# Attention, feed-forward and routed experts in one kernel: where the first block's weights and keys are made ready

## The chip, the cores and the metric

The kernel runs on one core of a Trainium2 chip. The metric is the device time of one execution in microseconds, the median of three runs. A core has five engines that run side by side, each through its own list of instructions in order: TensorE (PE; matmuls, with weight loads as an own row, PEld), VectorE (DVE), ScalarE (ACT), GpSimd (POOL) and SyncE (SP), which here only issues transfers. Results of matmuls land in PSUM, eight banks of 128 partitions by 512 words; everything else lives in SBUF.

## The reference, cut to what matters

```python
# q, k, v: 8 batches x 8 heads x 576 positions x 64
k_p = k.reshape(B, H, 72, 8, D).mean(axis=3)      # keys and values pooled by 8
v_p = v.reshape(B, H, 72, 8, D).mean(axis=3)
attn = softmax(q @ k_p.T / 8)                     # 576 x 72 for each batch and head
x = heads_joined(attn @ v_p)                      # 4608 tokens x 512
h = x @ w_in                                      # w_in: 512 x 2048
g = where(h >= 1, h, where(h <= -1, 0, (h + 1) ** 2 / 4))
y = g @ w_out                                     # w_out: 2048 x 512
# then each token goes to one of 8 experts (512 -> 1024 -> 512), chosen by y @ w_gate
```

`w_in` and `w_out` arrive as 64-bit floats, so that the kernel makes 32-bit words of them itself.

## The kernel before, in words

The 4608 tokens are 36 tiles of 128. They go through the feed-forward in ten blocks of 3, 4 (seven times), 3 and 2 tiles (`BLK`, L57). While one block is in its products, the attention of the next block's tiles is worked in between, unit by unit, from a list written out by hand (`weave`, L371; `slot`, L1032); the first block's three tiles go through attention ahead of everything (L982 to L1022, the head).

A product that has to be exact is made of three fast ones: each operand is split into a high part in the type `fp32r` and a low part, and high x high, high x low and low x high are added in PSUM. `f1` (L477) makes step m's first product: 12 matmuls into `ps0` or `ps1` (L483 to L485). Then VectorE clips (L490), ScalarE squares (L491), VectorE takes the larger (L495, `larger`), ScalarE copies the high part into `FG` (L496), and VectorE subtracts for the low part (L502, `lower`). `f2` (L505) makes the second product of step m for each tile: three matmuls (L511 to L513) with `FG` against `WO`, added over the 16 steps in banks `ps2` and following. `f1` runs two steps ahead of `f2` (`AHEAD`).

The weights are made ready during the head and the first block. `load_raw` (L403) fetches a slice of 64-bit words (512 KB) into one of six buffers `RB`; in all there are 16 slices of `w_in` and 16 of `w_out` (`order`, L446). A `tick` (L462) moves this on by one slice at each of its three stages. `convert_a` (L421) lets ScalarE scale the upper words into `WOF` or `DFI`. `convert_b` queues three steps for VectorE (`pend`, worked off by `mix`): shift left (L427), put in the lower word's upper bits (L428), put in the sign (L431), all three in SBUF. `convert_c` (L435) lets ScalarE copy the high part (L439) and GpSimd or VectorE subtract for the low part (L227, a helper's line); for `w_out` both parts are also stored to `wo_d` in memory (L442), 512 KB a slice. From the second block on `load_out` (L473) fetches them again for every step.

Keys and values: a batch has 8 slices each of 72 x 512 (144 KB), pooled by `pool_kv` into 72 x 64: one reduction on VectorE (L213) or three additions on GpSimd (L216 to L218). `u_kt` (L241) then turns the pooled keys with TensorE into `KBD`. Batch 0 is pooled in the head; batches from 1 on by `kv_step`, one slice at a time, through three buffers `RAW` that are refilled as they come free.

All transfers except those of `wo_d` into `WO` go through SP's queue in the order of the program; SP stands still at the first whose buffer isn't free.

Of the kernel before, what the change touches and what calls it, by code (L numbers as in the profile page):

```python
# [23 lines left out]
def attention_ffn_routed_experts_kernel(  # L24
# [44 lines left out]

    wo_d = dram.tile([KF, 128, 2, DM], F32R, name="wo_d")  # L70
# [36 lines left out]
    KP = at(4800, 512, SP_)  # L107
    YF = Y.rearrange("p t d -> p (t d)")
# [4 lines left out]
    NRB = len(RB)  # L113
    FR = fx(0, 512)
# [105 lines left out]
    banks = deque(ps[2:8])  # L220
# [16 lines left out]
    def flush():  # L237
        for _ in range(len(later)):
            later.popleft()()

# [116 lines left out]
    def kv_step(b, i):  # L357
        def f():
            n = (b - 1) * 2 * H + i
            pool_kv(b, i, RAW[n % 3], nc.vector)  # L360
            if n + 3 < (B - 1) * 2 * H:
                load_kv(1 + (n + 3) // (2 * H), (n + 3) % (2 * H), RAW[n % 3])
        return f
# [24 lines left out]
    I0 = 24  # L388
# [9 lines left out]
    units.insert(3, [units[3][0], lambda: u_kt(1)])  # L398
# [25 lines left out]
    def convert_b(i):  # L424
        dst, rb = cvt_dst(i)
        di = dst.bitcast(I32).rearrange("p (a x) -> p a x", a=8)
# [21 lines left out]
    n = FIRST  # L448
# [28 lines left out]
    def f1(j, m):  # L477
# [814 lines left out]
```

## Time and profile before

| | before |
|---|---|
| median of 3 runs | 1571.1 us (1569.75 to 1572.26) |
| profiled execution, own time | 1567.33 us |
| its span, first to last instruction | 1565.6 us |
| TensorE busy | 1456.0 us, 93% of the span |
| weight loads busy | 1185.2 us, 76% |
| VectorE busy | 796.5 us, 51% |
| ScalarE busy | 488.0 us, 31% |
| GpSimd busy | 220.2 us, 14% |
| granted TensorE clock, mean | 0.973 |
| transfers | 128 GB/s over the span |

The shares are means over a head, ten blocks of feed-forward (to about 1100 us) and the experts. A busy TensorE need not be one at its peak, as matmuls lie partly beside each other in its records. The granted clock is the share of full speed that the chip gave TensorE; full is 2.4 GHz and the lower level 1.2 GHz. In the rows below an arrow such as `<-DVE FG L502` names what ended an idle stretch.

### The profile page before, as it was taken

Reading aid. Unit: us, or ns where it says so; the run is one execution under the profiler, and the core shown is the slowest. Engines: PE = TensorE matmul, PEld = TensorE weight load, DVE = VectorE, ACT = ScalarE, POOL = GpSimd, SP = SyncE. Lnnn points to the kernel's source line nnn. Section 1 sums busy time; section 2 is a strip of 40 time slices with the busy share of each in tenths; the row PEclk is TensorE's granted clock in tenths of the full one; section 3 lists DMA queues with packets and bytes.
Section 4 is the critical chain, followed back from the end, with each engine's and each line's share of the span. In section 5 each row is a group of like instructions: output and inputs, shape, how many; then the busy total and the mean of one; then the engine's idle time right before and its main releaser. Section 6 shows DMA issues by size and latency. Waiting matters only on the chain.

```text
span 1565.6 us, 19805 instructions
## 1 busy us (share of the span) xinstructions
PE 1456.0 (93%) x7419; PEld 1185.2 (76%) x7419; DVE 796.5 (51%) x1561; ACT 488.0 (31%) x900; POOL 220.2 (14%) x218
## 2 busy tenths in 40 slices
PE   4677799899999999999999999898899999999697
PEld 3566577678778778778778788787788888888585
DVE  6798766545656654664764444434422222212326
ACT  5345332333333333333333333234211111111334
POOL 4222100000101001001000010102222110111112
PEclk9789999999999999999999999999999999999899
DMA  8466336525737637547456265877152110110413
GB/s 227 150 213 206 135 108 123 119 83 128 119 117 120 125 100 101 139 137 91 126 122 99 75 109 106 196 180 137 41 158 72 55 42 26 48 48 28 147 41 142
DMA packets 102631, 177.55 MB, mean 113 GB/s; under 512 B 46610, under 2 KB 54949, under 8 KB 102512
## 3 DMA queue, kind: packets, MB, share of 16 engines
q10 hardware_dynamic: 21552, 75.79, 24.4%
q1 hardware_dynamic: 73392, 79.93, 18.2%
q0 software_dynamic: 7568, 20.33, 4.0%
q8 instruction: 64, 1.05, 0.3%
q14 instruction: 55, 0.45, 0.1%
HBM read 171.32 MB, written 28.29 MB: 128 GB/s over the span
## 4 chain that ended last, share of the span: by engine, by line
PE 77%; DVE 9%; DMA 6%; issue 3%; ACT 2%; POOL 1%; another core or an unknown queue 1%; SPq 0%; ACTq 0%; DVEq 0%; POOLq 0%
PE ps L483 8%; PE ps L511 7%; PE ps L485 7%; PE ps L484 7%; PE ps L513 7%; PE ps L512 7%; PE ps L853 4%; PE ps L854 4%; PE ps L855 4%; PE ps L868 4%; PE ps L869 4%; PE ps L870 4%; PE ps L339 2%; PE ps L284 2%; DVE FX L428 2%
## 5 line engine op out<-in xcount | busy, mean ns | idle before, releaser
L511 PE MATMUL ps<-WO,FG 128*128 128x512 f32 x576 | 242.4, 421 | 23.5 <-ACT WO L439 11.2
L483 PE MATMUL ps<-XT,W 128*128 128x512 f32 (+2 forms) x640 | 252.2, 394 | 12.6 <-DVE FG L502 12.0
L484 PE MATMUL ps<-XT,W 128*128 128x512 f32 (+2 forms) x640 | 240.1, 375 | 3.0 <-DVE XT L345 3.0
L485 PE MATMUL ps<-XT,W 128*128 128x512 f32 (+2 forms) x640 | 240.2, 375 | 0.7 <-POOL W L227 0.7
L491 ACT ACTIVATE FX<-FX,half 128x512 f32<-128x512 f32 (+2 forms) x152 | 104.0, 684 | 418.5 <-DVE FX L490 407.4
L512 PE MATMUL ps<-WO,FG 128*128 128x512 f32 x576 | 230.5, 400 | 3.7 <-POOL WO L227 2.8
L513 PE MATMUL ps<-WO,FG 128*128 128x512 f32 x576 | 229.6, 399 | 0.0
L490 DVE TENSOR_SCALAR FX<-ps 128x512 f32<-128x512 f32 (+2 forms) x152 | 96.5, 635 | 183.0 <-PE ps L485 183.0
L859 DVE SCALAR_TENSOR_TENSOR FG<-ps,FG 128x512 fp32r<-128x512 f32 (+1 forms) x64 | 43.2, 675 | 220.1 <-ACT FG L858 220.1
L511 PEld LDWEIGHTS ps<-WO,FG 128*128 128x128 f32 x576 | 111.0, 193 | 55.0 <-issue 13.7
L483 PEld LDWEIGHTS ps<-XT,W 128*128 128x128 f32 x640 | 123.2, 193 | 36.1 <-DVE FG L502 13.9
L485 PEld LDWEIGHTS ps<-XT,W 128*128 128x128 f32 x640 | 123.1, 192 | 20.7 <-POOL W L227 1.4
L484 PEld LDWEIGHTS ps<-XT,W 128*128 128x128 f32 x640 | 123.6, 193 | 19.9 <-DVE XT L345 3.9
L496 ACT ACTIVATE FG<-ps 128x512 fp32r<-128x512 f32 (+2 forms) x160 | 88.7, 554 | 148.1 <-DVE ps L495 136.8
L512 PEld LDWEIGHTS ps<-WO,FG 128*128 128x128 f32 x576 | 111.2, 193 | 26.0 <-POOL WO L227 4.2
L513 PEld LDWEIGHTS ps<-WO,FG 128*128 128x128 f32 x576 | 110.6, 192 | 25.1
L495 DVE TENSOR_TENSOR ps<-FX,ps 128x512 f32<-128x512 f32 (+2 forms) x152 | 97.4, 641 | 55.6 <-ACT FX L491 54.4
L502 DVE TENSOR_TENSOR FG<-ps,FG 128x512 fp32r<-128x512 f32 (+2 forms) x160 | 100.7, 630 | 39.5 <-ACT FG L496 39.5
L858 ACT ACTIVATE FG<-ps 128x512 fp32r<-128x512 f32 (+1 forms) x64 | 37.4, 584 | 261.8 <-PE ps L855 261.3
L318 POOL TENSOR_TENSOR AT<-AT,ssm 128x576 f32<-128x576 f32 x36 | 42.6, 1186 | 478.9 <-DVE ssm L311 411.1
L853 PE MATMUL ps<-XT,W 128*128 128x512 f32 (+1 forms) x256 | 99.1, 387 | 0.0
L854 PE MATMUL ps<-XT,W 128*128 128x512 f32 (+1 forms) x256 | 98.7, 386 | 0.0
(229 smaller groups left out, 2287.0 us busy)
## 6 DMA issues: line engine op xcount, KB each, us to landing
WO<-wo_d ACTq DMA_DIRECT2D x144, 512.0 KB
AT<-in_moe_w_dram SPq DMA_DIRECT2D x10, 2048.0 KB
AT<-in_moe_w_dram SPq DMA_DIRECT2D x14, 1024.0 KB
AT<-in_v_dram SPq DMA_DIRECT2D x60, 144.0 KB
AT<-in_q_dram SPq DMA_DIRECT2D x32, 256.0 KB
wo_d<-WO SPq DMA_DIRECT2D x16, 512.0 KB
AT<-in_k_dram SPq DMA_DIRECT2D x56, 144.0 KB
yrow_d<-Y SPq DMA_DIRECT2D x7, 1032.0 KB
```

Of the source, the lines that this page charges most:

```text
L483: nc.tensor.matmul(o, wi(m, 0, c), xh, start=(c == 0), stop=False)
L484: nc.tensor.matmul(o, wi(m, 0, c), xl, start=False, stop=False)
L485: nc.tensor.matmul(o, wi(m, 1, c), xh, start=False, stop=(c == KD - 1))
L490: nc.vector.tensor_scalar(r, o, -1.0, 1.0, op0=ALU.max, op1=ALU.min)
L491: nc.scalar.activation(out=r, in_=r, func=ACTF.Square, scale=0.5, bias=half)
L495: nc.vector.tensor_tensor(out=o, in0=r, in1=o, op=ALU.max)
L502: nc.vector.tensor_tensor(out=gl, in0=o, in1=r32(gh), op=ALU.subtract)
L511: nc.tensor.matmul(o, gh, WO[:, g % 4, 0], start=(m == 0), stop=False)
L512: nc.tensor.matmul(o, gh, WO[:, g % 4, 1], start=False, stop=False)
L513: nc.tensor.matmul(o, gl, WO[:, g % 4, 0], start=False, stop=(m == KF - 1))
L853: nc.tensor.matmul(o, e1(0)[:, c, ms], xh, start=(c == 0), stop=False)
L854: nc.tensor.matmul(o, e1(0)[:, c, ms], xl, start=False, stop=False)
```

## The change

In words: keys of batches 0 and 1 are no longer pooled by reductions and then turned; 64 plain fp32 matmuls a batch against the unit matrix (`u_kp`) add and turn them in one, and ScalarE copies the sums into `KBD`. Batch 1's keys come in pairs through two new buffers `PAIR`; its values are pooled on GpSimd. Bank `ps5` becomes `CV`: the word being joined stands there between the three steps of a conversion. For the first block, `larger` writes the activations unsplit (`G32`), the second products are one plain fp32 matmul with the unsplit `WOF`, and `w_out` is neither copied nor split nor stored in two parts: the unsplit 256 KB go to `w32_d`. In the second block each step loads its slice from there, splits it on ScalarE and VectorE, uses it and stores both parts to `wo_d`, from which the third block on reads as before. The head issues its transfers and units in another order, a tick queues VectorE's three steps together with ScalarE's first and finishes a slice two ticks behind instead of three, and batch 2's pooling starts two units later.

```diff
+    w32_d = dram.tile([KF, 128, DM], F32, name="w32_d")
+    PAIR = [at(3264 + 1024 * i, 1024, SP_) for i in range(2)]
+    G32 = [WG.rearrange("p e d -> p (e d)")[:, 3072 + GN * i:3072 + GN * (i + 1)] for i in range(2)]
+    G32.append(at(6336, GN))
-    banks = deque(ps[2:8])
+    CV = ps[5]
+    banks = deque(ps[2:5] + ps[6:8])
+    def u_kp(b, c, raw):
+        pb = bank()
+        raw = raw.rearrange("p (a r d) -> p a r d", a=2, r=8)
+        for r in range(8):
+            for i in range(2):
+                nc.tensor.matmul(pb[64 * i:64 * i + 64, 0:SP_], raw[:, i, r], ident[0:SP_, 0:SP_],
+                                 start=(r == 0), stop=(r == 7))
+        nc.scalar.activation(out=KBD[b][0:64, c, 0:SP_], in_=pb[0:64, 0:SP_], func=ACTF.Copy)
+        nc.scalar.activation(out=KBD[b][64:128, c, SP_:2 * SP_], in_=pb[64:128, 0:SP_],
+                             func=ACTF.Copy)
...
-            pool_kv(b, i, RAW[n % 3], nc.vector)
+            pool_kv(b, i, RAW[n % 3], nc.vector if b > 1 else nc.gpsimd)
+    def load_pair(c):
+        for i in range(2):
+            load_kv(1, 2 * c + i, PAIR[c % 2][:, 512 * i:512 * (i + 1)])
+    def pair_step(c):
+        def f():
+            u_kp(1, c, PAIR[c % 2])
+            if c < 2:
+                load_pair(c + 2)
+            for n in ((9, 10), (8,))[c - 2] if c > 1 else ():
+                load_kv(1, n, RAW[n % 3])
+        return f
-    I0 = 24
+    I0 = 27
-    units.insert(3, [units[3][0], lambda: u_kt(1)])
...
     def convert_b(i):
-        pend.append(lambda: nc.vector.tensor_scalar(di, di, 3, None, op0=ALU.logical_shift_left))
+        di, ci = (x.bitcast(I32).rearrange("p (a x) -> p a x", a=8) for x in (dst, CV))
+        pend.append(lambda: None)
+        pend.append(lambda: nc.vector.tensor_scalar(ci, di, 3, None, op0=ALU.logical_shift_left))
         pend.append(lambda: nc.vector.scalar_tensor_tensor(
-            out=di, in0=rb[:, :, :, 0], scalar=29, in1=di, op0=ALU.logical_shift_right,
+            out=ci, in0=rb[:, :, :, 0], scalar=29, in1=ci, op0=ALU.logical_shift_right,
             op1=ALU.bitwise_or))
         pend.append(lambda: nc.vector.scalar_tensor_tensor(
-            out=di, in0=rb[:, :, :, 1], scalar=-2 ** 31, in1=di, op0=ALU.bitwise_and,
+            out=di, in0=rb[:, :, :, 1], scalar=-2 ** 31, in1=ci, op0=ALU.bitwise_and,
             op1=ALU.bitwise_or))
     def convert_c(i):
-        hi, lo = (WO[:, m % 4, 0], WO[:, m % 4, 1]) if o else (wi4(m, 0), wi4(m, 1))
+        if o:
+            nc.sync.dma_start(out=w32_d[m], in_=dst)
+            return
+        hi, lo = wi4(m, 0), wi4(m, 1)
         nc.scalar.activation(out=hi, in_=dst, func=ACTF.Copy)
-        low_part(lo, dst, hi, nc.vector if o and m % 3 else nc.gpsimd)
-        if o:
-            nc.sync.dma_start(out=r32(wo_d[m]), in_=r32(WO[:, m % 4]))
+        low_part(lo, dst, hi)
     def tick():
-        mix(3)
-        if n > 1:
-            more_raw(n - 2 + NRB)
-        for f, i in ((convert_c, n - 3), (convert_a, n), (convert_b, n - 1)):
+        mix(4)
+        if n > 0:
+            more_raw(n - 1 + NRB)
+        for f, i in ((convert_c, n - 2), (convert_a, n), (convert_b, n)):
+    def load_32(m):
+        nc.scalar.dma_start(out=WOF[m % 4], in_=w32_d[m])
+    def split_out(m):
+        nc.scalar.activation(out=WO[:, m % 4, 0], in_=WOF[m % 4], func=ACTF.Copy)
+    def split_low(m):
+        low_part(WO[:, m % 4, 1], WOF[m % 4], WO[:, m % 4, 0], nc.vector)
+        nc.sync.dma_start(out=r32(wo_d[m]), in_=r32(WO[:, m % 4]))
...
         def larger():
+            if j == 0:
+                nc.vector.tensor_tensor(out=G32[m % 3], in0=r, in1=o, op=ALU.max)
+                if m == KF - 1:
+                    load_32(0)
+                return
             nc.vector.tensor_tensor(out=o, in0=r, in1=o, op=ALU.max)
             nc.scalar.activation(out=gh, in_=o, func=ACTF.Copy)
-            if g + 1 >= KF and g + 1 < len(steps):
+            if j == 1:
+                split_out(m)
+                if m + 1 < KF:
+                    load_32(m + 1)
+            if g + 1 >= 2 * KF and g + 1 < len(steps):
                 load_out(g + 1)
         def lower():
             nc.vector.tensor_tensor(out=gl, in0=o, in1=r32(gh), op=ALU.subtract)
+            if j == 1:
+                split_low(m)
...
     def f2(j, m):
+            if j == 0:
+                nc.tensor.matmul(o, G32[m % 3][:, ts], WOF[m % 4], start=(m == 0), stop=(m == KF - 1))
+                continue
...
-        for i in range(8):
-            head_pool(i, nc.gpsimd if i in (1, 3, 5) else nc.vector)
-        u_kt(0)
+        for c in range(4):
+            u_kp(0, c, wgp[:, 1024 * c:1024 * (c + 1)])
+        load_pair(0)
+        load_pair(1)
-        kv = deque(kv_step(1, i) for i in range(2 * H))
+        kv = deque([pair_step(c) for c in range(4)] + [kv_step(1, i) for i in range(H, 2 * H)])
-        banks.extend(ps[2 + HEAD:8])
+        banks.extend(ps[6:8])
```

## Rows read from the trace of the kernel before

**Rows 1.** Busy time by stretch: us, then each engine, clock, transfers' share, GB/s

```profile
0.00:37.00 37.00, 18.48 (x112) 14.71 (x112) 23.31 (x45) 19.39 (x72) 17.80 (x34) 0.94 0.86 225
37.00:61.00 24.00, 13.55 (x43) 11.83 (x44) 18.23 (x27) 7.30 (x14) 5.51 (x4) 0.57 0.55 164
61.00:190.00 129.00, 99.42 (x508) 79.87 (x507) 111.92 (x193) 56.39 (x108) 32.39 (x30) 0.90 0.57 181
190.00:302.00 112.00, 104.92 (x536) 83.10 (x537) 69.21 (x127) 35.93 (x66) 7.75 (x7) 0.97 0.52 120
256.00:284.00 28.00, 27.38 (x143) 21.60 (x142) 17.81 (x28) 7.71 (x14) 3.11 (x3) 1.00 0.78 86
```

**Rows 2.** The chain of waits, 0 to 330 us, its shares by line

```profile
by line: DVE FX L428 7.7%; DMA AT<-in_v_dram 7.0%; issue 6.3%; DVE AT L213 4.9%; PE ps L483 4.8%; PE ps L485 4.4%; PE ps L484 4.4%; PE ps L511 4.0%; DMA AT<-in_k_dram 3.8%; PE ps L512 3.8%; PE ps L513 3.8%; DVE FX L431 3.7%; DVE FX L427 3.0
```

**Rows 3.** Waits of TensorE, 0 to 345 us: total, times, longest

```profile
PE ps L483 <- DVE FG L502: 12.0, 4, 6.3
PE ps L511 <- ACT WO L439: 11.2, 8, 3.9
```

**Rows 4.** VectorE's groups, 61 to 190 us: busy us, mean ns, idle before

```profile
L427 DVE TENSOR_SCALAR FX<-FX 128x512 int32<-128x512 int32 x25 | 13.0, 521 | 0.0
L428 DVE SCALAR_TENSOR_TENSOR FX<-WG,FX 128x512 int32<-128x512 int32 x12 | 12.4, 1031 | 0.1
...
L213 DVE TENSOR_REDUCE VS<-AT 72x64 f32<-72x512 f32 x8 | 8.4, 1044 | 0.0
L502 DVE TENSOR_TENSOR FG<-ps,FG 128x384 fp32r<-128x384 f32 x15 | 8.2, 546 | 0.0
...
L227 DVE TENSOR_TENSOR WO<-FX,WO 128x512 fp32r<-128x512 f32 x10 | 6.9, 691 | 5.1 <-ACT WO L439 5.1
...
L431 DVE SCALAR_TENSOR_TENSOR FX<-AT,FX 128x512 int32<-128x512 int32 x4 | 2.8, 688 | 0.1
```

**Rows 5.** Single lines of VectorE, 20 to 190 us: ns min/median/max

```profile
L427 DVE TENSOR_SCALAR FX<-FX x32: 405/417/1427, 28.8 to 176.2; 128x512 int32<-128x512 int32 x32
L428 DVE SCALAR_TENSOR_TENSOR FX<-WG,FX x15: 675/692/1741, 43.1 to 167.3; 128x512 int32<-128x512 int32 x15
L345 DVE SCALAR_TENSOR_TENSOR XT<-ps,XT x14: 406/424/425, 28.4 to 177.2; 128x256 fp32r<-128x256 f32 x14
L490 DVE TENSOR_SCALAR FX<-ps x10: 543/548/681, 50.8 to 189.7; 128x384 f32<-128x384 f32 x8, 128x512 f32<-128x512 f32 x2
```

**Rows 6.** Timeline of GpSimd and VectorE near 45 us: start, duration

```profile
45.20 1.71 POOL L227 TENSOR_TENSOR W<-FX,W 128x512 fp32r<-128x512 f32 x1 [3.63 <-ACT W L439]
...
45.81 1.65 DVE L428 SCALAR_TENSOR_TENSOR FX<-WG,FX 128x512 int32<-128x512 int32 x1
```

**Rows 7.** Timeline of TensorE: neighbouring first products, then neighbouring second products

```profile
65.80 0.33 PE L485 MATMUL ps<-XT,W 128*128 128x384 f32 x1
65.97 0.33 PE L483 MATMUL ps<-XT,W 128*128 128x384 f32 x1
...
220.14 0.40 PE L511 MATMUL ps<-WO,FG 128*128 128x512 f32 x1
...
220.38 0.39 PE L512 MATMUL ps<-WO,FG 128*128 128x512 f32 x1
```

**Rows 8.** The gate's line L544, plain fp32, whole span: ns min/median/max

```profile
L544 PE MATMUL ps<-WG,WGT x80: 379/592/597, 218.6 to 1101.0; 128*8 128x512 f32 x56, 128*8 128x384 f32 x16, 128*8 128x256 f32 x8
```

**Rows 9.** Timeline of TensorE, the start of the first block

```profile
37.20 0.69 PE L483 MATMUL ps<-XT,W 128*128 128x384 f32 x1 [0.63 <-ACT XT L344]
...
54.21 0.69 PE L483 MATMUL ps<-XT,W 128*128 128x384 f32 x1 [6.31 <-DVE FG L502]
...
61.16 0.80 PE L511 MATMUL ps<-WO,FG 128*128 128x512 f32 x1
```

**Rows 10.** The chain of waits, 250 to 290 us: start, us, what

```profile
252.59 9.39 DMA AT<-in_k_dram
...
274.90 12.49 DMA AT<-in_v_dram
```

More of the change, by code (lines that the diff above doesn't have):

```diff
@@ L113, in attention_ffn_routed_experts_kernel @@
     NRB = len(RB)
+    GN = blocks[0][1] * 128
+    G32 = [WG.rearrange("p e d -> p (e d)")[:, 3072 + GN * i:3072 + GN * (i + 1)] for i in range(2)]
+    G32.append(at(6336, GN))
     FR = fx(0, 512)
@@ L425, in convert_b @@
         dst, rb = cvt_dst(i)
-        di = dst.bitcast(I32).rearrange("p (a x) -> p a x", a=8)
-        pend.append(lambda: nc.vector.tensor_scalar(di, di, 3, None, op0=ALU.logical_shift_left))
+        di, ci = (x.bitcast(I32).rearrange("p (a x) -> p a x", a=8) for x in (dst, CV))
+        pend.append(lambda: None)
+        pend.append(lambda: nc.vector.tensor_scalar(ci, di, 3, None, op0=ALU.logical_shift_left))
         pend.append(lambda: nc.vector.scalar_tensor_tensor(
-            out=di, in0=rb[:, :, :, 0], scalar=29, in1=di, op0=ALU.logical_shift_right,
+            out=ci, in0=rb[:, :, :, 0], scalar=29, in1=ci, op0=ALU.logical_shift_right,
             op1=ALU.bitwise_or))
         pend.append(lambda: nc.vector.scalar_tensor_tensor(
-            out=di, in0=rb[:, :, :, 1], scalar=-2 ** 31, in1=di, op0=ALU.bitwise_and,
+            out=di, in0=rb[:, :, :, 1], scalar=-2 ** 31, in1=ci, op0=ALU.bitwise_and,
             op1=ALU.bitwise_or))
@@ L968, in attention_ffn_routed_experts_kernel @@
     with tc.manual_schedule():
-        pre = [WG[0:SP_, i] for i in range(8)]
-        raw0 = pre + RAW + [FX[0:SP_, 512 * i:512 * (i + 1)] for i in range(1, 5)] + [JK[0:SP_]]
+        wgp = WG.rearrange("p e d -> p (e d)")[0:SP_]
+        raw0 = [WG[0:SP_, i] for i in range(8)] + RAW + [
+            FX[0:SP_, 512 * i:512 * (i + 1)] for i in range(1, 5)] + [KP]
         nc.scalar.dma_start(out=WGT, in_=w_gate.rearrange("(c p) e -> p c e", p=128))
@@ L984, in attention_ffn_routed_experts_kernel @@
             load_kv(0, i, raw0[i])
+        more_raw(0)
         load_q(1)
-        hu[0][0]()
         for i in range(H, 2 * H):
             load_kv(0, i, raw0[i])
-        for i in range(3):
-            more_raw(i)
-        for i in range(8):
-            head_pool(i, nc.gpsimd if i in (1, 3, 5) else nc.vector)
-        for i in range(8, 13):
-            head_pool(i, nc.gpsimd)
-        for i in range(3):
-            load_kv(1, i, RAW[i])
-        hu[1][0]()
-        u_kt(0)
-        hu[0][1]()
-        hu[0][2]()
-        hu[1][1]()
-        hu[1][2]()
-        for i in range(13, 16):
-            head_pool(i, nc.vector)
-        hu[2][0]()
+        hu[0][0]()
+        more_raw(1)
+        more_raw(2)
+        for c in range(4):
+            u_kp(0, c, wgp[:, 1024 * c:1024 * (c + 1)])
         for i in range(3, NRB):
             more_raw(i)
+        tick()
+        hu[1][0]()
+        for i in (8, 10, 12, 14):
+            head_pool(i, nc.gpsimd)
+        mix(4)
+        head_pool(9, nc.vector)
+        hu[0][1]()
+        head_pool(11, nc.vector)
+        hu[0][2]()
+        head_pool(13, nc.vector)
+        hu[1][1]()
+        head_pool(15, nc.vector)
+        load_pair(0)
+        load_pair(1)
+        hu[1][2]()
+        hu[2][0]()
         flush()
+        tick()
         hu[2][1]()
@@ L1018, in attention_ffn_routed_experts_kernel @@
             flush()
-            if i % 2 == 1 and ticks[0] < CAHEAD + 4:
+            if i % 2 == 1 and ticks[0] < CAHEAD + 3:
                 tick()
-            if i > 3 and kv:
-                kv.popleft()()
-        while ticks[0] < CAHEAD + 4:
+        while ticks[0] < CAHEAD + 3:
             tick()
         banks.clear()
-        banks.extend(ps[2 + HEAD:8])
+        banks.extend(ps[6:8])
         steps = [(j, m) for j in range(NB) for m in range(KF)]
```

## The prediction, made before the changed kernel was run

> **What bounds the kernel now.** I read the engine shares first, then busy time by stretch, then one engine's lines inside the stretch that looked wrong, then who waits for whom there. TensorE is busy 93% of the whole span, but that is an average over unlike stages. By stretch [rows 1] the second block (190 to 302 us) holds TensorE at 104.9 of 112 us, and there only fewer or faster matmuls could help. The first block (61 to 190 us) takes 129 us for three tiles, against 112 us for four, and has TensorE at 99.4, VectorE at 111.9 of 129 and a granted clock of 0.90; the 24 us before it have VectorE at 18.2 and a clock of 0.57. The reader is to see that in these 153 us VectorE is the fuller engine. The chain of waits agrees [rows 2]: over the first 330 us its largest single item is VectorE's L428, with L213, L431 and L427 of the same engine behind it. TensorE's own waits [rows 3] name it again: 12.0 us for FG from L502 and 11.2 us for WO from L439, which itself stands behind VectorE's conversion. So what counts is what the change takes off VectorE before 190 us, and what it adds to TensorE there and to the transfers of the second block.
>
> Times are made against the profiled execution, 1567.33 us with a span of 1565.6; the three runs have a median of 1571.1, which is 3.8 more, and I move the answer by the same difference.
>
> **The change part by part, first block (61 to 190 us).** VectorE [rows 4] (the 27 rows of this view add up to 124 us where the stretch has 111.9 busy, so some 0.07 of each instruction lies beside the next, and I take that off):
> - Values of batch 1 pooled on GpSimd instead: 8 of L213 at 1.044 go, 8 x 0.97 = 7.8 us. Keys of batch 2 start two units later and the inserted key unit is gone; counting the list of units, 5 instead of 8 of them fall into this block: 3 x 0.97 = 2.9 us move to the second block, where VectorE is at 69 of 112.
> - Low halves of the first block's activations (L502) go: 15 x 0.47 = 7.0 us.
> - Low halves of w_out on VectorE (L227) go: 10 x 0.61 = 6.1 us, and the 5.1 us that VectorE stood idle in front of them waiting for ScalarE's copy.
> - Conversions stay, 25 in this stretch (L427, L428 and L431, seven rows by source buffer of which three are shown; busy 13.0 + 12.4 + 7.8 + 2.7 + 9.0 + 8.2 + 2.8 = 55.9 us). What is new is that a PSUM bank holds the word between the three steps. Undisturbed, an L428 takes 0.68 to 0.69, disturbed up to 1.74 [rows 5]. At 45.81 one took 1.65 while GpSimd's L227 ran from 45.20 [rows 6]. L345, the same instruction with one input in PSUM, stayed within 0.406 to 0.425 in all its 14 runs [rows 5]. So steps two and three should stay at their undisturbed 0.68 and 0.69. Step one now writes PSUM. No row shows that; it lies between the 0.417 median of today's form (L427's mean is 0.521 with its disturbed ones) and L490's 0.681 with 512 elements read from PSUM [rows 4, 5]. I take 0.68, the one nearest in kind. That makes 25 x (0.68 + 0.68 + 0.69) = 51.3, a gain of 4.6 us; with the low end for step one it is 11.2, and if PSUM shields nothing and step one still grows, 25 x (0.68 - 0.52) = 4 us are lost.
>
> The sum for VectorE is 7.8 + 2.9 + 7.0 + 6.1 + 5.1 + 4.6 = 33.5, so a stage bound by VectorE as now would last 129 - 33.5 = 95.5 us.
>
> The Trainium skill speaks against this part in "VectorE: DVE Perf Modes", under why PSUM operands drop a tier: one-source fp32 work runs at double rate only from SBUF to SBUF. By that rule step one costs the 0.68 that the row of L490 gave; without it the sum would be 6.6 us better. Its page "SBUF — State Buffer", under who interferes with whom, has a VectorE instruction with one SBUF input and at single rate never wait for GpSimd: by that the 4 us of loss can't come, L345's 14 runs agree, and no row shows an integer step with a word in PSUM.
>
> TensorE in the same stage. Matmuls of 384 columns start 0.17 us apart and of 512 columns 0.23 us apart [rows 7], while a record of the latter lasts 0.40; a record therefore ends some 0.165 us later than its column stream. L544, plain fp32 with 512 columns, has records of 0.592, so a stream of 0.427, and 80 records for 40 products: two each [rows 8]. A second product in plain fp32 should then cost 2 x 0.427 = 0.854 plus the 0.018 per record that the 0.231 spacing has over its own stream, 0.89 us. The three that it replaces take 3 x 0.231 = 0.69. For 16 x 3 products TensorE goes from 33.3 to 42.7 us: it gains work. First products: 16 x 12 x 0.172 = 33.0. Attention: the second block has 104.9 us busy and 16 x 24 x 0.231 = 88.7 in its products, so 16.2 at most for four tiles with the routing. Together 92 us. VectorE's 95.5 and TensorE's 92 now almost meet, and two engines that feed each other do not both run full: between 0 (VectorE's 95.5 already holds its 12 us of idle time) and 16 us (the 17 us that VectorE is idle today, once more) I put 8 on top. The stage then lasts some 103 us: **26 us less**, between 18 and 34.
>
> ScalarE (56.4 of 129 us) loses the copies of WO and FG, and GpSimd (32.4 of 129) takes 8 poolings, each surely under the 1.71 of a full 128x512 [rows 6]; both cost nothing as long as a pooling that waits for its values doesn't keep L227 behind it from the first products. Storing 256 KB instead of 512 KB per step takes 4.2 MB off a queue that moved 181 GB/s here.
>
> **Before the first block (0 to 61 us).** VectorE loses 8 poolings of batch 1's keys (8 x 0.97 = 7.8 us), which stood between the conversions from 29 to 45 us. TensorE gets 64 plain products per batch in their place. What ends last today [rows 9]: first products from 37.2, a hole of 6.31 us until 54.21 waiting for FG from L502, the first second product at 61.16. That hole goes, since a VectorE with less in its queue frees the bank sooner. Late next are batch 1's keys: TensorE now stands at u_kp until each pair has landed, with the value products and the first products of the block queued behind it. Counting on SP's queue up to the last pair: 4 of q (1.05 MB), 16 of batch 0 (2.36), 9 raw blocks (4.7), 8 keys (1.2), together 9.3 MB at the 225 GB/s of the first stretch, 41 us and 2 to 3 for the start: 44 us. Then the rest of the values and three first products at the slow clock, some 9 to 13 us: the first second product at 53 to 57. If only two pairs hold it up it is 49. I take 53: **8 us less**, between 4 and 12. In front of that u_kp(0) waits for keys that land one by one, where pooling on two engines kept pace; I count that inside these bounds, as the softmax of the first tiles still follows the same transfers.
>
> **Second block (190 to 302 us).** Added per step: a load of 256 KB on ScalarE's queue, a copy (0.62), a subtraction on VectorE (0.69) and a store of 512 KB on SP's queue; gone is the 512 KB load. Engines have room: VectorE 69 + 16 x 0.69 + 2.9 = 83 of 112, ScalarE 36 + 10. The transfers are the question. The load is issued one step (7.0 us) before ScalarE's copy waits for it, with the activations of the next step queued behind; before, it had three steps. And SP's stores stand ahead of the keys and values that VectorE pools. In 256 to 284 us the queues moved only 86 GB/s at a busy share of 0.78 [rows 1], 144 KB of keys or values took 9.4 to 12.5 us to land [rows 10], and the wait of TensorE for FG that this block has comes right behind. Per step the demand rises from about 0.9 to 1.15 MB. At 86 GB/s these 28 us carry 2.4 MB, 2.1 steps instead of 4: 13 us lost if nothing is buffered, and some 5 us of slack in the two steps between first and second product. So between -4 (the present hole goes) and +13; I take **4 us more**.
>
> Sum: -26 - 8 + 4 = -30; 1567.3 becomes 1537, and the median of runs 1571.1 - 30 = 1541. Everything after 302 us is the same work.
>
> **Rivals.**
> - TensorE becomes the bound: 92 us of work at the 0.90 clock of today's stage make 102, with the same 8 of friction 110 instead of 103, and the late keys leave 4 instead of 8 of the front: -19 - 4 + 4 = -19, 1552. For it: the plain products. Against it: a fuller engine has held a clock of 0.97 to 1.00 [rows 1].
> - Both engines overlap as well as in the second block and its transfers are hidden: 95.5 in the stage, 49 for the front, nothing lost later: -33.5 - 12 + 2 = -43.5, 1528. For it: two steps of slack between a first product and its use.
> - PSUM shields nothing, so the change doesn't do what it says to the conversions: 8.6 us worse than my sum, 1550. Against it: L345 [rows 5].
> - Slower than before: the second block is paced by its transfers. Place: ScalarE's wait for the unsplit weights, and SP's stores ahead of keys and values. It cancels 34 us of gain when 16 steps take 2.1 us more each, 9.1 instead of 7.0, which is when the queues move less than 1.15 MB / 9.1 us = 126 GB/s. With 86 GB/s over half the block, 8 steps of 13.4 instead of 7.0 lose 51 us: 1571 - 34 + 51 = 1588. For it: the 28 us above. Against it: 181 GB/s and 225 GB/s elsewhere, and 120 GB/s in this block is what it asked for, with a busy share of 0.52.
>
> **How the numbers follow.** Forecast 0.46 (1541, its own range 1531 to 1551); TensorE bound 0.18 (1552); everything overlaps 0.17 (1528); PSUM shields nothing 0.07 (1550); transfers of the second block 0.09, slower; 0.03 for a gain that is eaten just about whole. Faster by over 0.2% (some 3 us, which is what this kernel's runs can tell) 0.88, within it 0.03, slower 0.09. The range from 1522 to 1562 leaves out the slow case and the ends of the others.
>
> **What would show it.** Right: L428's and L431's longest runs near 0.7 us, L427's at 0.68; no L502 and no VectorE L227 for w_out before the second block; two records of about 0.59 for each second product of block 0; the first of them at about 53 us; the second block starting at about 156 with the clock near 1. Wrong: second products further apart than 0.9 us, TensorE waiting at u_kp beyond 45 us, or ScalarE waiting several us per step for the unsplit weights in the second block.

## The result, and the profile after

The changed kernel takes 1537.05 us, the median of four runs (1534.68 to 1538.44), against 1570.98 (1569.75 to 1572.26) for the kernel before on the same chip: 0.9782 of its time, 95% interval 0.9765 to 0.9799. The prediction was 1541 in 1531 to 1551. The profiled execution took 1536.88 us with a span of 1534.8, 30.8 less than the span before. Of all runs reported here one is left out of every figure: a run of the last experiment that took 3683.67 us where its other three took 1530 to 1533.

Where the 30.8 us lie is read from three marks: the first second product, and the evictions of the first and of the second block (the first `ACTIVATE Y<-ps` of each).

| us | first first product | first second product | first block evicted | second block evicted | from the first eviction to the end |
|---|---|---|---|---|---|
| before | 37.20 | 61.16 | 192.5 | 308.1 | 1373.1 |
| after | 40.99 | 54.92 | 161.6 | 273.1 | 1373.2 |

The evictions stand so in the two timelines, before and then after:

```profile
192.52 1.08 ACT L520 ACTIVATE Y<-ps 128x512 f32<-128x512 f32 x2
308.08 1.09 ACT L520 ACTIVATE Y<-ps 128x512 f32<-128x512 f32 x2
...
161.61 1.08 ACT L580 ACTIVATE Y<-ps 128x512 f32<-128x512 f32 x2
273.14 1.09 ACT L580 ACTIVATE Y<-ps 128x512 f32<-128x512 f32 x2
```

The first block is evicted 30.9 us earlier: 6.2 by the front, 24.7 by the stage behind it. The second block is 4.1 shorter in this pair of profiles, and the stretch behind it is 4.3 longer. That stretch has the same code in the thirteen profiles of this document that compute the whole result, and it took between 1257 and 1264 us in them, so its 4.3 says nothing of the change.

Busy time by stretch, after (columns as in [rows 1]), which stands against those rows; the third is the first block's stage, the fourth the second block:

```profile
0.00:37.00 37.00, 22.20 (x220) 19.24 (x220) 17.57 (x39) 19.72 (x75) 12.87 (x23) 0.90 0.88 230
37.00:61.00 24.00, 19.28 (x143) 15.84 (x144) 14.20 (x27) 8.87 (x19) 2.40 (x3) 0.80 0.52 155
55.00:161.60 106.60, 99.30 (x554) 68.32 (x555) 86.58 (x158) 46.32 (x89) 34.30 (x49) 0.98 0.61 185
161.60:273.10 111.50, 107.07 (x558) 84.57 (x557) 81.24 (x146) 43.59 (x82) 7.74 (x7) 1.00 0.64 166
```

The same two stages of the kernel before, cut at its own marks:

```profile
61.20:192.50 131.30, 101.72 (x518) 81.71 (x517) 113.02 (x194) 57.63 (x110) 32.39 (x30) 0.90 0.56 179
192.50:308.00 115.50, 108.42 (x552) 86.05 (x551) 70.22 (x128) 36.45 (x68) 7.75 (x7) 0.97 0.51 120
```

In the first block's stage VectorE goes from 113.0 to 86.6 us of work and the stage from 131.3 to 106.6: VectorE loses 26.4 and the stage 24.7, and what the stage is longer than VectorE's work stays, 18.3 before and 20.0 after. TensorE's busy time hardly moves, and the granted clock rises from 0.90 to 0.98.

VectorE's groups in the stage (columns as in [rows 4]):

```profile
L460 DVE TENSOR_SCALAR ps<-FX 128x512 int32<-128x512 int32 x25 | 17.1, 685 | 0.3
L461 DVE SCALAR_TENSOR_TENSOR ps<-WG,ps 128x512 int32<-128x512 int32 x12 | 8.3, 692 | 0.2
L464 DVE SCALAR_TENSOR_TENSOR FX<-WG,ps 128x512 int32<-128x512 int32 x12 | 8.1, 677 | 0.3
...
L218 DVE TENSOR_REDUCE AT<-AT 72x64 f32<-72x512 f32 x5 | 5.2, 1046 | 0.0
...
L535 DVE TENSOR_SCALAR FX<-ps 128x384 f32<-128x384 f32 x6 | 3.3, 551 | 4.6 <-PE ps L530 4.6
```

L460, L461 and L464 are the three steps of a conversion; their seven rows by source buffer add up to 51.5 us. Five poolings (L218) are left, as counted. The lower half of `w_out` and that of the activations are gone up to the second block's first steps. Single lines of VectorE, 10 to 165 us (columns as in [rows 5]):

```profile
L460 DVE TENSOR_SCALAR ps<-FX x32: 682/684/695, 15.3 to 150.9; 128x512 int32<-128x512 int32 x32
...
L461 DVE SCALAR_TENSOR_TENSOR ps<-WG,ps x15: 681/695/696, 36.6 to 143.0; 128x512 int32<-128x512 int32 x15
...
L464 DVE SCALAR_TENSOR_TENSOR FX<-WG,ps x15: 635/686/689, 37.4 to 143.8; 128x512 int32<-128x512 int32 x15
```

The longest of the second step was 1741 in [rows 5]; with the word in PSUM it is 696. TensorE's plain second products (L569):

```profile
L569 PE MATMUL ps<-FX,WG x66: 590/592/697, 54.9 to 159.8; 128*128 128x512 f32 x66
L569 PE MATMUL ps<-FX,AT x30: 590/592/595, 75.0 to 154.5; 128*128 128x512 f32 x30
```

96 records for 48 products, two each of 592 ns, as [rows 8] had them. The front, TensorE's timeline (to be held against [rows 9]):

```profile
40.99 0.69 PE L528 MATMUL ps<-XT,W 128*128 128x384 f32 x1
43.30 0.69 PE L529 MATMUL ps<-XT,W 128*128 128x384 f32 x1 [1.62 <-DVE XT L363]
...
53.09 0.76 PE L302 MATMUL ps<-AT 128*128 128x144 f32 x4 [1.34 <-ACT AT L293]
53.77 1.22 PE L253 MATMUL ps<-ident,AT 72*64 72x72 f32 x32
54.92 2.84 PE L569 MATMUL ps<-FX,WG 128*128 128x512 f32 x6
57.60 0.65 PE L302 MATMUL ps<-AT 128*128 128x144 f32 x4
```

The 6.31 us hole of [rows 9] is gone. Three plain products take 2.68 (54.92 to 57.60), 0.89 each. And by its waits (total, times, longest; 0 to 310 us) TensorE waits 0.9 us for the activations' lower half (in the second block) and none for `w_out`; what is left from [rows 3]'s view is the head's attention and transfers:

```profile
PE ps L302 <- ACT AT L293: 7.0, 2, 5.7
...
PE ps L253 <- DMA AT<-in_k_dram: 2.7, 2, 2.3
```

### The profile page after: what moved, and what is told of

Read it like the earlier page. It is cut to its first block, busy times and chain, and to the rows that moved or that the text cites. A ratio compares the mean times of both kernels' runs of the same rounds, so it can differ in the third digit from the quotient of the medians.

```text
span 1534.8 us, 20243 instructions
## 1 busy us (share of the span) xinstructions
PE 1458.4 (95%) x7619; PEld 1177.2 (77%) x7619; DVE 771.7 (50%) x1531; ACT 484.2 (32%) x896; POOL 212.6 (14%) x224
## 4 chain that ended last, share of the span: by engine, by line
PE 81%; DMA 7%; DVE 6%; issue 3%; ACT 1%; another core or an unknown queue 1%; POOL 1%; SPq 1%; ACTq 0%; DVEq 0%; POOLq 0%
PE ps L528 8%; PE ps L529 7%; PE ps L530 7%; PE ps L571 7%; PE ps L573 7%; PE ps L572 7%; PE ps L913 4%; PE ps L914 4%; PE ps L915 4%; PE ps L928 3%; PE ps L930 3%; PE ps L929 3%; PE ps L357 2%; PE ps L302 2%; DMA WO<-wo_d 1%
## 5 line engine op out<-in xcount | busy, mean ns | idle before, releaser
L571 PE MATMUL ps<-WO,FG 128*128 128x512 f32 x528 | 218.9, 415 | 9.4 <-DMA WO<-wo_d 9.4
L573 PE MATMUL ps<-WO,FG 128*128 128x512 f32 x528 | 208.2, 394 | 0.0
L572 PE MATMUL ps<-WO,FG 128*128 128x512 f32 x528 | 208.0, 394 | 0.0
L529 PEld LDWEIGHTS ps<-XT,W 128*128 128x128 f32 x640 | 123.1, 192 | 18.8 <-DVE XT L363 2.3
L530 PEld LDWEIGHTS ps<-XT,W 128*128 128x128 f32 x640 | 122.7, 192 | 19.2
L571 PEld LDWEIGHTS ps<-WO,FG 128*128 128x128 f32 x528 | 100.2, 190 | 36.1 <-issue 18.3
L547 ACT ACTIVATE FG<-ps 128x512 fp32r<-128x512 f32 (+2 forms) x144 | 81.0, 562 | 124.7 <-DVE ps L546 114.0
L546 DVE TENSOR_TENSOR ps<-FX,ps 128x512 f32<-128x512 f32 (+2 forms) x144 | 92.9, 645 | 54.1 <-ACT FX L536 54.1
L573 PEld LDWEIGHTS ps<-WO,FG 128*128 128x128 f32 x528 | 100.1, 190 | 23.0
L572 PEld LDWEIGHTS ps<-WO,FG 128*128 128x128 f32 x528 | 100.5, 190 | 17.2
L557 DVE TENSOR_TENSOR FG<-ps,FG 128x512 fp32r<-128x512 f32 (+2 forms) x144 | 92.0, 639 | 38.3 <-ACT FG L547 38.2
```

What stands on the lines that cost most here:

```text
L529: nc.tensor.matmul(o, wi(m, 0, c), xl, start=False, stop=False)
L530: nc.tensor.matmul(o, wi(m, 1, c), xh, start=False, stop=(c == KD - 1))
L571: nc.tensor.matmul(o, gh, WO[:, g % 4, 0], start=(m == 0), stop=False)
L572: nc.tensor.matmul(o, gh, WO[:, g % 4, 1], start=False, stop=False)
L573: nc.tensor.matmul(o, gl, WO[:, g % 4, 0], start=False, stop=(m == KF - 1))
```

## The experiments

The theory after the result was that TensorE, busy 99.3 of 106.6 us, had become the bound of the first block's stage and VectorE's list no longer counted. The rival was that VectorE still set it. Each run below is compared with the kernel before on its own chip; there the latter had medians of 1562 to 1563, not 1571, so ratios are what compares. A stretch is read from one profile of each kernel. "Stage" is from the first second product to the first block's eviction; 106.7 in the changed kernel.

**The words back in SBUF.**

```diff
-        di, ci = (x.bitcast(I32).rearrange("p (a x) -> p a x", a=8) for x in (dst, CV))
+        di, ci = (x.bitcast(I32).rearrange("p (a x) -> p a x", a=8) for x in (dst, dst))
```

> The changed kernel, with the word kept in SBUF between the three conversion steps, as before. Theory (the first block's stage, 106.6 us from the first second product to the eviction, is now bound by TensorE, 99.3 us busy, and VectorE with 86.6 has room): the long conversion steps of 1.4 to 1.8 us come back, VectorE's 51.5 us for 25 conversions become some 56 to 60, and the kernel loses only 0 to 3 us (1537 to 1540). Rival (VectorE's time still sets the stage, as it did before the change): all of it shows, 5 to 9 us (1542 to 1546).

Median 1547.83, ratio 0.9899 [0.9864, 0.9935]. The stage, its busy times:

```profile
57.80:176.30 118.50, 106.22 (x557) 71.66 (x554) 96.66 (x158) 46.40 (x90) 41.71 (x49) 0.93 0.55 167
```

VectorE's steps, 55 to 176 us:

```profile
L460 DVE TENSOR_SCALAR FX<-FX 128x512 int32<-128x512 int32 x25 | 18.5, 742 | 0.0
L461 DVE SCALAR_TENSOR_TENSOR FX<-WG,FX 128x512 int32<-128x512 int32 x12 | 11.9, 988 | 0.2
L464 DVE SCALAR_TENSOR_TENSOR FX<-Y,FX 128x512 int32<-128x512 int32 x9 | 10.0, 1116 | 0.3
```

Single lines of its steps one and three, 10 to 180 us (ns min/median/max):

```profile
L460 DVE TENSOR_SCALAR FX<-FX x32: 409/421/1520, 15.2 to 165.9; 128x512 int32<-128x512 int32 x32
...
L464 DVE SCALAR_TENSOR_TENSOR FX<-WG,FX x15: 640/691/1649, 38.1 to 158.9; 128x512 int32<-128x512 int32 x15
```

GpSimd's groups in the stage of this kernel:

```profile
L233 POOL TENSOR_TENSOR W<-FX,W 128x512 fp32r<-128x512 f32 x12 | 17.1, 1429 | 49.4 <-ACT W L476 49.4
L221 POOL TENSOR_TENSOR AT<-AT 72x256 f32<-72x256 f32 x8 | 7.6, 955 | 9.0 <-DMA AT<-in_v_dram 9.0
```

And the same two groups in the changed kernel:

```profile
L233 POOL TENSOR_TENSOR W<-FX,W 128x512 fp32r<-128x512 f32 x12 | 15.3, 1276 | 46.7 <-ACT W L476 46.7
L221 POOL TENSOR_TENSOR AT<-AT 72x256 f32<-72x256 f32 x8 | 5.8, 728 | 7.1 <-DMA AT<-in_v_dram 7.1
```

In SBUF step one is faster when alone (421 against 684) and slower on the mean (742 against 685). VectorE works 96.7 us instead of 86.7, GpSimd 41.7 instead of 34.3 for the same 49 instructions: both lose. That the two collide is seen step by step: all 22 of this kernel's 96 steps that took over 0.9 us lie beside a GpSimd instruction in time, and those that lie beside none took at most 0.69. In the changed kernel 60 of the 96 lie beside one, and none took over 0.70. The stage grows by 11.8 though nothing on TensorE is touched: against the theory, and more than the rival's 5 to 9.

**The first block split as before**: second products in three, `w_out` split and stored in the first block, the second block loading both parts.

```diff
-            nc.sync.dma_start(out=w32_d[m], in_=dst)
-            return
+        hi, lo = (WO[:, m % 4, 0], WO[:, m % 4, 1]) if o else (wi4(m, 0), wi4(m, 1))
...
-                nc.tensor.matmul(o, G32[m % 3][:, ts], WOF[m % 4], start=(m == 0), stop=(m == KF - 1))
-                continue
...
```

> The changed kernel with the first block's second products split into three fast matmuls again, w_out split and stored in two parts there, the second block fetching them as before; keys by TensorE and words in PSUM stay. TensorE has 9.4 us less to do in the stage, VectorE some 13 more (L502 7.0, low parts of w_out 6.1) and the waits on ScalarE's copy. Theory (with plain products TensorE is the bound, without them VectorE is again, at 86.6 + 13 = 100 us and its waits): the stage stays within 103 to 112 us, the kernel at 1534 to 1543. First rival (plain products pay 9.4 us and buy nothing, since TensorE alone counts): the stage falls to 97 to 99, 1528. Second rival (unsplit products are where the gain came from): the stage goes up by 15 or more, 1552.

Median 1545.76, ratio 0.9886 [0.9851, 0.992]. The stage, its busy times:

```profile
57.00:175.40 118.40, 99.26 (x611) 80.03 (x608) 100.23 (x181) 59.22 (x117) 41.13 (x54) 0.96 0.63 200
```

VectorE has the 100 us that the theory gave it, but the stage is above the theory's 112 and short of the second rival's 15 more; the first rival falls. Leaving the first block unsplit is worth 11.7 us of stage although a plain product is the slower one on TensorE (0.89 against 0.69 us for the three). The second block takes 107.1, 4.4 less than in the changed kernel.

**Batch 1's values pooled by VectorE.**

```diff
-            pool_kv(b, i, RAW[n % 3], nc.vector if b > 1 else nc.gpsimd)
+            pool_kv(b, i, RAW[n % 3], nc.vector)
```

> The changed kernel with batch 1's values pooled by reductions on VectorE instead of additions on GpSimd: 8 x 0.97 = 7.8 us more for VectorE in the first block's stage. Theory (TensorE bound): 0 to 2 us (1537 to 1539). Rival (VectorE bound): 6 to 8 us (1543 to 1545).

Median 1541.19, ratio 0.986 [0.9825, 0.9896]. The stage, its busy times:

```profile
54.70:167.50 112.80, 101.64 (x556) 69.41 (x555) 94.01 (x166) 46.42 (x89) 22.63 (x25) 0.95 0.57 175
```

VectorE +7.3, stage +6.1. The conversions stay at 51.5 us, so the eight poolings are what was added.

**Fewer plain products**: TensorE relieved, VectorE untouched.

```diff
+                if t == 2:
+                    if m == 0:
+                        nc.tensor.matmul(o, G32[m % 3][:, ts], WOF[m % 4], start=True, stop=True)
+                    continue
```

> The changed kernel without 15 of the 16 second products of the first block's third tile (its 128 tokens get only step 0's share, so their experts may differ and the end of the kernel is not compared; the stage from the first second product to the eviction is). TensorE has 15 x 0.87 = 13 us less of 99.3. Theory (TensorE bound): the stage of 106.6 us shrinks by 8 to 13 us. Rival (VectorE, or the round trip between the two engines, sets it): by 0 to 3 us.

One run. The stage, its busy times:

```profile
54.50:160.40 105.90, 91.34 (x537) 64.44 (x534) 86.66 (x158) 46.25 (x89) 34.34 (x49) 0.97 0.62 187
```

TensorE is busy 8.1 us less, and the stage gains 0.8 where the theory had 8 to 13. The granted clock is 0.97 instead of 0.98; going by the reordered front below, that may hide some 2 us of gain (an estimate). The theory falls even so: TensorE's work does not set this stage.

**The changed kernel again**, on another chip.

> The changed kernel once more, as the reference for the kernels of this call and the last. Both theories: as when it was first timed, a ratio of 0.978 to the kernel before, and a stage of 106 to 107 us from the first second product of the first block to its eviction.

Median 1534.64 (1524.78 to 1537.01), ratio 0.9798 [0.9754, 0.9842]; stage 106.5, second block 108.8, span 1532.2. The ratio holds. The run with a second store below has the same code up to the first eviction and 106.5 as well, so three executions of this stage lie within 0.2 us.

**The front in another order**: the third tile's queries ahead of batch 0's values, and the first two tiles' score steps ahead of part of VectorE's poolings and conversions.

```diff
+        hu[0][0]()
...
+        hu[0][1]()
+        hu[0][2]()
...
```

> The changed kernel with two moves ahead of the first block: the third tile's queries are asked for before batch 0's values (they were late, and TensorE waited 5.7 us for their copy), and the first tile's two score steps come before VectorE's first conversion and pooling. Theory (the front of 55 us follows the softmax of the three tiles on ScalarE, and what comes later shifts with it): first products at 37 to 39 instead of 41.0, first second product at 51 to 53 instead of 54.9, the kernel 2 to 4 us shorter. Rival (VectorE's conversions, not the softmax, set the front): 0.

Median 1536.98, ratio 0.9835 [0.9808, 0.9863]. First products at 40.30 and the first second product at 54.99 (40.30 and 54.77 in the changed kernel on this chip): no gain in the front, against the theory. The stage, its busy times:

```profile
55.00:159.80 104.80, 97.82 (x556) 66.93 (x555) 86.59 (x158) 46.22 (x89) 34.35 (x49) 1.00 0.62 188
```

It is 1.9 shorter with the same work on VectorE. What differs is the clock: from 70 to 80 us, behind a wait of TensorE of about 2 us for a pair of keys that both kernels have, it is 1.00 here and 0.83 in the changed kernel:

```profile
70.00:80.00 10.00, 10.00 (x75) 7.72 (x72) 5.51 (x11) 4.26 (x9) 2.31 (x4) 1.00 0.66 219
...
70.00:80.00 10.00, 10.00 (x73) 7.91 (x69) 4.10 (x8) 2.83 (x7) 1.50 (x3) 0.83 0.54 170
```

The missing 0.17 of these 10 us is 1.7 us of TensorE at full speed, close to what the stage gained. So just behind that wait TensorE's speed seems to count; one pair of profiles doesn't show more.

**The first block's clip on ScalarE**: VectorE relieved.

```diff
+        if j == 0:
+            nc.scalar.activation(out=r, in_=o, func=ACTF.Relu, scale=-0.5, bias=half)
+            nc.scalar.activation(out=r, in_=r, func=ACTF.Relu, scale=-1.0, bias=one)
+            nc.scalar.activation(out=r, in_=r, func=ACTF.Square)
...
```

> The changed kernel with the first block's clip moved off VectorE: L535 (16 x 0.47 = 7.5 us) goes, ScalarE makes the same value with two more steps (some 16 x 1.2 us; it has 46 of 106.6 us busy). The earlier runs refuted that TensorE alone is the bound. Theory now (VectorE's list of instructions sets the stage, 51 of 58 us busy while the conversions last, TensorE close behind): the stage shrinks by 4 to 7 us. Rival (the two engines bind together or the round trip through ScalarE does): 0 to 2 us, or longer.

Median 1536.42, ratio 0.9827 [0.9803, 0.9851]. The stage, its busy times:

```profile
55.50:157.00 101.50, 98.24 (x556) 68.09 (x553) 80.90 (x145) 59.40 (x115) 34.38 (x49) 0.98 0.63 193
```

VectorE 5.8 less, stage 5.2 less, with TensorE's work much as it was. This is the counterpart of the fewer products, and it names VectorE. TensorE now has 3 us of idle time left in the stage. The profile's span is 1530.1, but the runs don't separate from the changed kernel's.

**The kernel before, with only the words in PSUM.**

```diff
-    banks = deque(ps[2:8])
+    CV = ps[5]
+    banks = deque(ps[2:5] + ps[6:8])
...
-        pend.append(lambda: nc.vector.tensor_scalar(di, di, 3, None, op0=ALU.logical_shift_left))
+        pend.append(lambda: nc.vector.tensor_scalar(ci, di, 3, None, op0=ALU.logical_shift_left))
...
```

> The kernel before with one part of the change alone: the word of a conversion stands in a PSUM bank between its three steps (five banks instead of six for the head, two instead of three for the attention in the first block). Taking this part out of the changed kernel cost its stage 11.7 us, where the prediction had 4.6. Theory (the part is worth what it saves VectorE in each kernel: there the 25 conversions fall from 55.9 to 51.5 us busy): 4 to 6 us faster than the kernel before. Rival (the part is worth more than its VectorE time, since the long steps also hold up what stands behind them): 8 to 12 us faster.

Median 1556.69, ratio 0.9956 [0.993, 0.9982]. The stage and the second block, busy times:

```profile
60.10:187.30 127.20, 101.92 (x517) 81.57 (x517) 109.87 (x194) 57.58 (x110) 29.20 (x30) 0.89 0.58 184
...
187.30:294.30 107.00, 104.79 (x553) 83.95 (x552) 70.42 (x128) 36.59 (x68) 7.76 (x7) 1.00 0.50 129
```

VectorE 3.1 less, GpSimd 3.2 less for the same 30 instructions, stage 4.1 less. The second block, whose code is that of the kernel before, takes 107.0, not 115.5. The theory's 4 to 6 us fit the stage. The medians are 6.8 us apart and the two profiles 14.1, of which 8.5 lie in the second block, whose hole is looked at below.

**Batch 1's keys pooled by VectorE in the head, as before.**

```diff
-        kv = deque([pair_step(c) for c in range(4)] + [kv_step(1, i) for i in range(H, 2 * H)])
+        kv = deque(kv_step(1, i) for i in range(2 * H))
...
+            if i > 3 and kv:
+                kv.popleft()()
...
```

> The changed kernel with batch 1's keys pooled by VectorE's reductions ahead of the first block and then turned, as before; batch 0's stay with TensorE, the values with GpSimd. Theory (the prediction's: 8 x 0.97 = 7.8 us of VectorE stood in the front and made TensorE's hole of 6.3 us there): the first second product at 58 to 62 instead of 54.8, and the stage behind it 0 to 3 us shorter, since TensorE has 4.9 us less there. Rival (the hole closed because of the words in PSUM and the unsplit activations): the first second product stays within 1 us of 54.8 and the kernel is not longer.

Median 1540.49, ratio 0.9874 [0.9823, 0.9925]. TensorE's front:

```profile
49.08 0.69 PE L530 MATMUL ps<-XT,W 128*128 128x384 f32 x1 [7.06 <-DVE XT L363]
...
59.58 2.74 PE L570 MATMUL ps<-FX,WG 128*128 128x512 f32 x6
```

The hole is back, 7.06 us, behind the low part of the tokens from VectorE (L363), and the first second product 4.7 later. The stage is 105.9, 0.8 less than with TensorE's sums: batch 1's key sums by TensorE pay in the front alone. (The span, 1534.2, does not show the 4.7: the second block ended 2.2 us later than the changed kernel's, and the last stages gave these back too; the runs have a median of 1540.)

**A second store in the second block**, another 512 KB a step on SP's queue.

```diff
+        nc.sync.dma_start(out=r32(wx_d[m]), in_=r32(WO[:, m % 4]))
...
```

> The changed kernel with every store of the second block issued twice, the second into memory that nothing reads: 512 KB more per step on SP's queue, ahead of the keys and values. Prediction's term (transfers of the second block are partly on the path; it charged 4 us for 256 KB more per step): the second block, 108.8 to 111.5 us between the evictions in two executions, grows by 6 to 12 us. Theory now (what the second block asks of the queues hides behind TensorE): 0 to 3 us.

Median 1538.15, ratio 0.9853 [0.9807, 0.99]. The second block, and its fullest stretch of 40 us:

```profile
161.00:276.00 115.00, 109.48 (x558) 86.75 (x557) 81.23 (x146) 43.97 (x83) 7.74 (x7) 0.97 0.83 231
232.00:272.00 40.00, 35.98 (x165) 28.18 (x163) 25.11 (x39) 13.41 (x24) 2.11 (x2) 0.91 1.01 241
```

The queues carry 231 GB/s instead of 166 and the block takes 114.9 us. The ten profiles with the edit and one store have 108.3 to 111.5, so a whole extra store a step costs 3.4 to 6.6 us, one wait of TensorE of 3.5 us among it: more than the theory's 0 to 3, and at most the low end of the prediction's term.

**Batch 2's pooling three units earlier**, so that eight of its poolings fall into the first block's stage again, as before, instead of five.

```diff
-    I0 = 27
+    I0 = 24
```

> The changed kernel with batch 2's pooling three units earlier, as before the change: three more poolings of 0.97 us on VectorE in the first block's stage and three fewer in the second block. Theory (VectorE sets the stage): the stage grows by 2 to 4 us from 106.6, the second block is the same. Rival (these poolings come behind the last conversions, where TensorE sets the pace): 0 to 1 us.

Median 1537.14, ratio 0.9843 [0.9796, 0.9891]. The stage, its busy times:

```profile
55.20:165.40 110.20, 101.44 (x556) 69.02 (x555) 89.33 (x161) 46.24 (x89) 34.40 (x49) 0.97 0.61 183
```

VectorE has 2.6 us more work, and the stage is 3.5 us longer.

**The front's order and the clip on ScalarE together.**

> The changed kernel with the two edits that shortened the stage, put together: the front reordered (stage 104.8 instead of 106.5 in its run) and the clip on ScalarE (101.5). Theory (both take from VectorE's list where it is full): the stage at 99.5 to 101.5 and the first eviction at 155 to 157 instead of 161.3, so 4 to 6 us faster than the changed kernel, at a ratio of 0.975 to 0.979. Rival (with the clip gone TensorE binds): the stage stays at 101.5 and the ratio at 0.98.

Median 1531.74 of three runs, the lowest 1530.01, ratio 0.9794 [0.974, 0.9848]; first second product 56.19, stage 102.3 with VectorE at 80.5. The stage and the first eviction, at 158.5, miss the expected 99.5 to 101.5 and 155 to 157: what the other order had gained was not VectorE's work, which is 86.6 in it as in the changed kernel. The eviction is 3.1 earlier than in the changed kernel; the interval does not separate the two, so no version is shown to be faster.

All stages in one table, worked out from the busy times by stretch:

| stage of | us | VectorE busy | the rest | TensorE busy | clock |
|---|---|---|---|---|---|
| before | 131.3 | 113.0 | 18.3 | 101.7 | 0.90 |
| before, words in PSUM | 127.2 | 109.9 | 17.3 | 101.9 | 0.89 |
| words in SBUF | 118.5 | 96.7 | 21.8 | 106.2 | 0.93 |
| split as before | 118.4 | 100.2 | 18.2 | 99.3 | 0.96 |
| values by VectorE | 112.8 | 94.0 | 18.8 | 101.6 | 0.95 |
| batch 2 earlier | 110.2 | 89.3 | 20.9 | 101.4 | 0.97 |
| changed kernel | 106.7 | 86.7 | 20.0 | 99.4 | 0.98 |
| second store | 106.5 | 86.7 | 19.9 | 99.5 | 0.98 |
| keys by VectorE | 105.9 | 88.8 | 17.1 | 96.7 | 0.97 |
| fewer plain products | 105.9 | 86.7 | 19.2 | 91.3 | 0.97 |
| front in another order | 104.8 | 86.6 | 18.2 | 97.8 | 1.00 |
| front and clip | 102.3 | 80.5 | 21.8 | 99.3 | 0.97 |
| clip on ScalarE | 101.5 | 80.9 | 20.6 | 98.2 | 0.98 |

The stage is VectorE's work and 17 to 22 us. TensorE's busy time, between 91 and 106, does not order it, and neither does the clock order the rest: 18.3 us at 0.90, 20.0 at 0.98, 18.2 at 1.00. The ratios tell less. Of the runs that take one part out of the changed kernel only those with the words in SBUF and with the first block split stand clear of both intervals of the changed kernel; the others rest on their stages.

## Why the prediction was right, and which terms were not

- **The bound.** It took VectorE's list as what sets the first block, before and (with 95.5 against TensorE's 92) narrowly after. The runs show it: taking 5.8 us off VectorE shortens the stage by 5.2, taking 8.1 off TensorE by 0.8.
- **The first block, -26.** Measured -24.7. VectorE's work fell by 26.4 where the terms without idle time made 28.4; the stage's rest is 20.0, which is what the forecast's 8 of friction on 12 of idle time amounts to. That the 8 fit is luck: they were the middle between 0 and 16, put there because TensorE would be nearly as full as VectorE, and with 8.1 us less on TensorE the rest is still 19.2. Conversions came to 51.5 for 51.3, batch 2's poolings to 5 as counted, a plain product to 0.89.
- **The mis-sized term: 4.6 us for the words in PSUM.** As a difference between the two profiles it is right (55.9 to 51.5), and alone it is worth 4.1. But in the changed kernel taking it back costs 11.8 us of stage: the change gives GpSimd eight more poolings (49 instructions in the stage instead of 30), and the conversions collide more, 61.7 us instead of the 55.9 before. The nearest run to the rival "PSUM shields nothing" (8.6 us more, 1550) stands at 0.9899, which is 1555 on the first chip; it isn't quite that kernel, as its word is in SBUF. That the bank does shield is shown by the steps; before the result the bet was thinner than it reads, since of the 14 runs of L345 only four lay beside a GpSimd instruction. Likewise unsplit products cost 11.7 to undo, values 6.1, batch 2's start 3.5. These make 33 us for a gain of 24.7: singly undone, parts that help each other are counted twice. That this is the reason is argued; no run undid two of them together.
- **The front, -8.** Measured -6.2, with a wrong reason in it. I put the pairs of batch 1's keys into the front and took their transfers (44 us) as what is late next. The diff also takes the line `if i > 3 and kv: kv.popleft()()` out of the head, so the pair steps run in the first block's slots, from 53.8 us on; TensorE waited 2.3 us for one at 69. A wait at u_kp beyond 45 us was named as a sign of being wrong: it came, and was small. What is late next is the attention of the first tiles: first products start 3.8 us later (40.99) than before. TensorE's sums of batch 0's keys, from 5.74 to 14.05, are the likely reason, not a shown one: the run with batch 1's keys by VectorE keeps them and has 41.33, the one of the kernel before with words in PSUM lacks them and has 38.12. What was right is that VectorE's key poolings made the hole: with them back it is 7.06 us.
- **The second block, +4.** Its sign looks wrong, -4.1, and isn't. In the kernel before a hole of TensorE stood in it:

```profile
289.08 0.79 PE L483 MATMUL ps<-XT,W 128*128 128x512 f32 x1 [4.25 <-DVE FG L502]
```

  VectorE stood at the value slice that took 12.49 us [rows 10], and FG behind it. The next matmuls start 0.43 apart instead of 0.23, and the granted clock was 0.77 from 289 to 296. The same code without the hole took 107.0 (words in PSUM) and, in the kernel split as before, 107.1. The ten profiles with the edit and one store have 108.3 to 111.5. So the edit costs some 1 to 4.5 us, inside the forecast, and the hole's going hid it. This block was to start at about 156 and starts at 161.6: the front is 1.9 us later than forecast, and the stage, which runs from mark to mark (131.3 before, not the 129 reckoned with), 3.7 longer. Whether the kernel before has its hole in most executions stays open: only one was profiled.
- **The slower rival** asked for queues below 126 GB/s. They carried 166, and 231 when a second store asked for more. The 86 GB/s of [rows 1] was no ceiling.
- **TensorE as the bound** (1552) fell with the fewer products. Its busy share, 93% of the stage, had made me believe it after the result; its records lie beside each other, and 8 us less of them bought 0.8.
- **The sum, -30.** Measured -30.8 between the profiles and -33.9 between the medians. That it came so close is in part luck. The front and the first block gave 3.1 us less than forecast, the second block 8 more, and the stretch behind it took 4.3 back in this pair of profiles, where the forecast had the same time.

Not settled: what share of the gain is the clock's (0.90 to 0.98 in the stage). The reordered front comes nearest to a test, with VectorE's work the same, the clock 0.02 higher and the stage 1.9 us shorter, but it is one pair of profiles, and over all stages the rest does not follow the clock. Open as well are what makes up the 17 to 22 us beside VectorE's work, and what the head's new order, the ticks and batch 0's key sums are worth, as no run undid these alone.

## What to carry to other kernels

Take the busy time of each engine in the stage, not in the span, and test which one sets it by relieving one engine at a time; a TensorE busy for 93% of a stage need not be its bound. Where two engines stretch each other's instructions, price a move of work from one to the other together with what it collides with, as the parts' worths don't add. A transfer that an in-order engine stands at costs what is queued behind it, so look there for holes before asking how many bytes are moved.

## What the runs showed of the hardware

- A word kept in PSUM between integer steps takes the collision with GpSimd away on both sides. VectorE's longest step was 0.70 us, beside a GpSimd instruction or not, against 1.65 in SBUF in the otherwise equal kernel, where every step over 0.9 us lay beside one; and GpSimd's same 49 instructions took 34.3 instead of 41.7. The Trainium skill, "SBUF — State Buffer", under who interferes with whom, says that a VectorE instruction with at most one SBUF input and outside the two-port modes doesn't contend with GpSimd; the trace agrees, here for integer steps too.
- The shift in place in SBUF is the quicker form by its median (0.42 us against 0.68 into PSUM) and the dearer by its mean (0.74 against 0.685 in the first block's stage).
- A hole of 4 us in TensorE's work was followed by a granted clock of 0.77 over the next 7 us, with matmuls at first 0.43 apart instead of 0.23, as at the lower level (1.2 GHz): the wait cost more than itself. A wait of 2.3 us in the changed kernel was followed by 0.83 from 70 to 80 us, one of 2.1 us in the reordered front by 1.00.
